# Seven block products for eight in the first two batches, behind the attention of all four

## The chip, the cores and the metric

The kernel runs on one core of one Trainium2 chip. The metric is the time of one execution on the device in microseconds (us), as the median of several runs. TensorE is called PE below, its weight loads PEld, VectorE DVE, ScalarE ACT, GpSimd POOL; SP (SyncE) issues the DMAs.

## What is computed

Three layers in a row, in float32: attention with a sigmoid in the softmax's place (4 batches, 12 heads, 448 positions, head width 64), a gated layer, and a layer with `h - tanh(h)`:

```python
scores = np.matmul(q, k.transpose(0, 1, 3, 2)) / 8 - np.log(448)
x = np.matmul(1 / (1 + np.exp(-scores)), v)        # as [1792 tokens, 768]
xn = x / np.sqrt(np.mean(x * x, -1) + 1e-6) * rms_g
g = xn @ w_gate                                    # 768 -> 1536
y = (g / (1 + np.exp(-g)) * (xn @ w_val)) @ w_out  # 1536 -> 768
h = y @ w_in2                                      # 768 -> 2048
out = (h - np.tanh(h)) @ w_out2                    # 2048 -> 768
```

The weights come as 64-bit floats.

## The kernel before, in words

Activations lie with features on the 128 partitions and the 448 tokens of a batch in the free dimension, one "unit" of 128 x 448 floats per chunk of features. Phase A is `w_gate` ("Ag") and `w_val` ("Av"), B is `w_out`, C is `w_in2`, D is `w_out2`. A float32 operand is split into a rounded part h (float32r) and the rest l, and a product is three matmuls hh + hl + lh of 128 x 128 weights and 448 columns. A **job** is one DMA of six 128 x 128 weight blocks (`jobs`, L285 to L339).

Batches 0 and 1 run all four phases first, then batches 2 and 3 (`BATCHES`). In the first half every job takes raw weights from memory (`load`, L349), rebuilds float32 out of the two halves of a 64-bit number (`fields`, `join`, L464 to L474), splits them (L479, L483) and stores them for the second half (`put`, L488). Phases A and C of the first half are plain block products for each batch (`job_units`, L925): 1440 matmuls. In the second half, A and C take two batches and two output chunks together in Strassen's manner with Winograd's sums (`seven_units`, L871): seven products of half the depth, each in a PSUM bank of its own, where the plain way has eight; DVE adds the banks into SBUF units (`plus`, L879; `done`, L884). That is 1260 matmuls. B and D are plain in both halves; their inner dimension is done in groups of four chunks (`GR`), and after each group DVE adds the bank to a sum that is held in SBUF (L829 to L835).

Attention: in batches 0 and 1 two heads go as a pair, values as plain float32 matmuls on the float32 sigmoids (`pair_av`, L616). In batches 2 and 3 each sigmoid is written to PSUM, split by ACT and DVE into h and l (`head_parts`, L652), and multiplied in seven float32r matmuls a head (`head_av`, L668). Batch 0's attention stands first; batch 1's runs beside the first jobs of batch 0, those of batches 2 and 3 beside the rest of the first half (`beside`, L1049).

The order on each engine is set by a planner (`Plan`, L61): work is listed with its reads, writes and a cost per engine, and is placed in time greedily, oldest first among what can start within `SOON` of the earliest. Buffers are slots of pools with a limit per kind (L240). Each engine runs its list in order, so a row that waits holds up the rows behind it. PSUM has 8 banks.

Of the kernel before, what the change touches and what calls it, by code (L numbers as in the profile page):

```python
# [8 lines left out]
F32 = mybir.dt.float32  # L9
# [12 lines left out]
P = 128  # L22
KM, KF1, KF2 = DM // P, FF1 // P, FF2 // P
EPS = 1e-6
NB = 6
ALONE = 3
GR = 4
# [4 lines left out]
N_WARM = 7  # L32
LOADS = [5, 6]
BEHIND = 2
MM = 190
SOON = 300
WINDOW = 500
N_UNIT, N_MOE, N_RAW, N_WT = 83, 44, 2, 7
N_AGAIN = 4
BACK = 3  # L40
BATCHES = ((0, 1), (2, 3))
# [3 lines left out]
ORDER_1_OUT = [(k, m) for g in range(KF1 // GR) for m in range(KM) for k in range(g * GR, (g + 1) * GR)]  # L45
ORDER_2 = [(k, m) for m in range(KF2) for k in range(KM)]
ORDER_2_OUT = [(k, m) for g in range(KF2 // GR) for m in range(KM) for k in range(g * GR, (g + 1) * GR)]
# [13 lines left out]
class Plan:  # L61
# [5 lines left out]
    WINDOW = WINDOW  # L67

    def __init__(self, room):
        self.room, self.work = room, []  # L70

    def add(self, engines, run, reads=(), writes=(), stream=None, after=0):

        n = len(self.work)
        self.work.append((engines, run, tuple(reads), tuple(writes), stream, after))
        for s, _ in (*reads, *writes):
            if not s.uses or s.uses[-1] != n:
                s.uses.append(n)

    def issue(self):  # L80
# [70 lines left out]
        while len(issued) < n_work:  # L151
# [3 lines left out]
            for n in waiting:  # L155
# [3 lines left out]
                if stream and streams[stream][stream_at[stream]] != n:  # L159
                    continue  # L160
                t_place = places(n)
# [15 lines left out]
            finish, start, n, e, ns, uses_port = min((c for c in cands if c[1] <= soonest), key=lambda c: c[2])  # L177
# [33 lines left out]
def tile_sigmoid_attention_moe_moe(  # L211
# [21 lines left out]
    cv_p = ctx.enter_context(tc.tile_pool(name="cv", bufs=2))  # L233
    v_p = ctx.enter_context(tc.tile_pool(name="v", bufs=2))
# [6 lines left out]
        "unit": (N_UNIT, {"moe": N_MOE, "kept": 24, "a": 40, "s": 14, "qk": 8, "qkr": 4, "acc": 12, "x": 12, "tmp_m": 8, "tmp_a": 4, "sq": 2, "rstd": 3,  # L241
                          "xs": 42, "tmp_s": 8, "tmp_x": 8}),
        "wt": (N_WT, {"raw": N_RAW, "whl": N_WT - N_RAW, "again": N_AGAIN, "op": 4}),
        "cv": (2, {"cv": 2}),
        "v": (2, {"v": 2}),
# [21 lines left out]
    def act(n, psum=False, ptr=False):  # L267
        return {"ACT": ((51 if psum else 93) + n / 1.2 + 93 * ptr, False)}

    def dve(n, two=True, psum=True, fast=False):  # L270
        return {"DVE": (66 + n / 0.96 / (2 if fast else 1), fast or (two and not psum))}

    def pool(n):
        return {"POOL": (110 + n * 2.16, True)}
# [4 lines left out]
    g_sb = const.tile([P, KM], F32, name="g_sb")  # L279
    id_sb = const.tile([TK, TK], F32, name="id_sb")  # L280
# [5 lines left out]

    def job(ph, bs, src, i, order):
        jobs.append((ph, bs, src, i, order[i * NB:(i + 1) * NB]))

    def group_a(bs, ms):  # L290
        for m in ms:
            job("Ag", bs, w_gate, m, ORDER_1)
            job("Av", bs, w_val, m, ORDER_1)

    def group_c(bs, ms):
        for m in ms:
            job("C", bs, w_in2, m, ORDER_2)

    PG = KM * GR // NB
    PAIRS = {"Ag": (w_gate, "A"), "Av": (w_val, "A"), "C": (w_in2, "C")}  # L300

    def second(ph, bs, g):
        for i in range(g * PG, (g + 1) * PG):
            job(ph, bs, *((w_out, i, ORDER_1_OUT) if ph == "B" else (w_out2, i, ORDER_2_OUT)))


    bs = BATCHES[0]
    for b in bs:
        group_a((b,), range(ALONE))
    group_a(bs, range(ALONE, GR))  # L310
    for g in range(KF1 // GR):
        ahead = range((g + 1) * GR, min((g + 2) * GR, KF1))
        group_a(bs, ahead[:1])
        second("B", bs, g)
        group_a(bs, ahead[1:])
    group_c(bs, range(GR))
    for g in range(KF2 // GR):
        ahead = range((g + 1) * GR, min((g + 2) * GR, KF2))
        group_c(bs, ahead[:1])
        second("D", bs, g)  # L320
        group_c(bs, ahead[1:])
# [810 lines left out]
```

## Time and profile before

| | us |
|---|---|
| median of 3 runs (1142.49 to 1144.13) | 1143.16 |
| the profiled execution | 1141.8 |
| its span, first to last instruction | 1140.0 |
| PE busy | 1123.2 |
| DVE busy | 759.7 |
| ACT busy | 407.0 |
| POOL busy | 173.0 |

A busy PE is one that has a matmul in flight. The stretches of the span: to 66 us batch 0's attention, to 126 us batch 1's with the first products, to 604 us the other two attentions among the first half's products, to 673 us the rest of phase D of batches 0 and 1, then the second half.

### The profile page before, as it was taken

Reading aid. Unit: us, or ns where it says so; the run is one execution under the profiler, and the core shown is the slowest. Engines: PE = TensorE matmul, PEld = TensorE weight load, DVE = VectorE, ACT = ScalarE, POOL = GpSimd, SP = SyncE. Lnnn points to the kernel's source line nnn. Section 1 sums busy time; section 2 is a strip of 40 time slices with the busy share of each in tenths; the row PEclk is TensorE's granted clock in tenths of the full one; section 3 lists DMA queues with packets and bytes.
Section 4 is the critical chain, followed back from the end, with each engine's and each line's share of the span. In section 5 each row is a group of like instructions: output and inputs, shape, how many; then the busy total and the mean of one; then the engine's idle time right before and its main releaser. Section 6 shows DMA issues by size and latency. Waiting matters only on the chain.

```text
span 1140.0 us, 15501 instructions
## 1 busy us (share of the span) xinstructions
PE 1123.2 (99%) x5706; PEld 986.9 (87%) x5706; DVE 759.7 (67%) x1303; ACT 406.9 (36%) x760; POOL 173.0 (15%) x136
## 2 busy tenths in 40 slices
PE   8999999999999999999999999999999999999998
PEld 5456788989889899898999899999999899999987
DVE  3576966675675987677575978738648897455542
ACT  4776534344443554444432422212202333212100
POOL 0001110121121221010121310111202302121200
PEclk9999999999999999999999999999999999999999
DMA  6778747666666575656549454424434434343322
GB/s 180 224 226 272 273 146 237 228 221 228 217 203 240 173 239 196 223 211 224 177 169 303 152 177 157 158 94 158 145 113 143 146 125 139 117 156 116 125 84 97
DMA packets 85245, 205.56 MB, mean 180 GB/s; under 512 B 11825, under 2 KB 49841, under 8 KB 85169
## 3 DMA queue, kind: packets, MB, share of 16 engines
q1 hardware_dynamic: 85168, 204.57, 53.8%
q8 instruction: 45, 0.74, 0.3%
q14 instruction: 32, 0.25, 0.1%
HBM read 134.93 MB, written 69.60 MB: 179 GB/s over the span
## 4 chain that ended last, share of the span: by engine, by line
PE 90%; DVE 3%; DMA 2%; SPq 2%; ACT 1%; issue 1%; POOL 0%; DVEq 0%; ACTq 0%; POOLq 0%
PE ps L953 60%; PE ps L909 21%; PE ps L587 4%; SPq L534 2%; DMA unit<-in_qkt 1%; PE ps L681 1%; PE ps L680 1%; PE ps L626 1%; DMA wt<-in_w_gate 1%; DVE unit L808 0%; PE ps L678 0%; DMA wt<-in_w_val 0%; DVE unit L755 0%; PE ps L630 0%; ACT unit L277 0%
## 5 line engine op out<-in xcount | busy, mean ns | idle before, releaser
L953 PE MATMUL ps<-unit,wt 128*128 128x448 f32 x3240 | 670.1, 366 | 2.5 <-DVE unit L277 1.5
L953 PEld LDWEIGHTS ps<-unit,wt 128*128 128x128 f32 x3240 | 605.5, 188 | 59.8 <-issue 5.9
L909 PE MATMUL ps<-unit,wt 128*128 128x448 f32 x1260 | 256.9, 365 | 0.0
L909 PEld LDWEIGHTS ps<-unit,wt 128*128 128x128 f32 x1260 | 236.4, 188 | 19.3
L277 ACT CAST wt<-cv 128x384 fp32r<-128x384 f32 (+1 forms) x81 | 50.3, 628 | 207.3 <-POOL cv L408 54.0
L835 DVE TENSOR_TENSOR unit<-ps,unit 128x448 f32<-128x448 f32 x120 | 69.4, 617 | 77.0 <-PE ps L953 76.6
L881 DVE TENSOR_TENSOR unit<-ps,unit 128x448 f32<-128x448 f32 x140 | 83.1, 619 | 38.1 <-PE ps L909 36.7
L277 ACT COPY unit<-ps 128x448 f32<-128x448 f32 (+1 forms) x78 | 41.1, 533 | 182.3 <-PE ps L909 61.9
L485 POOL TENSOR_TENSOR wt<-cv,wt 128x768 fp32r<-128x768 f32 x29 | 56.1, 1934 | 262.4 <-DVE wt L277 77.8
L277 ACT CAST unit<-unit 128x448 fp32r<-128x448 f32 (+1 forms) x125 | 66.8, 566 | 63.5 <-DVE unit L775 14.2
L808 DVE TENSOR_TENSOR unit<-unit 128x448 fp32r<-128x448 f32 x110 | 80.0, 739 | 8.8 <-ACT unit L277 6.1
L587 PE MATMUL ps<-unit 64*128 64x448 f32 (+1 forms) x576 | 74.2, 392 | 3.3 <-DVE unit L277 2.5
L472 DVE SCALAR_TENSOR_TENSOR cv<-wt,zero 128x768 uint32<-128x768 uint32 x68 | 67.7, 996 | 11.3 <-POOL wt L485 8.4
L666 DVE TENSOR_TENSOR unit<-ps,unit 128x448 fp32r<-128x448 f32 (+1 forms) x96 | 57.8, 619 | 23.5 <-ACT unit L277 18.1
L587 PEld LDWEIGHTS ps<-unit 64*128 64x128 f32 (+1 forms) x576 | 50.1, 179 | 25.5 <-issue 10.6
L277 DVE CAST wt<-cv 128x768 fp32r<-128x768 f32 (+1 forms) x61 | 29.2, 478 | 61.4 <-PE ps L953 51.7
L597 ACT ACTIVATE ps<-ps 128x448 f32<-128x448 f32 (+1 forms) x96 | 48.4, 527 | 46.8 <-PE ps L587 46.7
L277 ACT CAST zero<-wt 128x768 f16<-128x768 bf16 x41 | 44.2, 1077 | 43.1 <-DMA wt<-in_w_out 12.3
L953 PE MATMUL ps<-unit 128*128 128x448 f32 x216 | 50.1, 380 | 2.9 <-DVE unit L759 1.6
L277 DVE CAST unit<-unit 128x448 fp32r<-128x448 f32 (+1 forms) x90 | 35.1, 390 | 22.9 <-DMA unit<-in_qkt 14.3
L953 PEld LDWEIGHTS ps<-unit 128*128 128x128 f32 x216 | 39.5, 188 | 12.1 <-issue 5.0
L597 ACT ACTIVATE unit<-ps 128x448 f32<-128x448 f32 (+1 forms) x96 | 45.5, 540 | 4.5 <-PE ps L587 3.7
(80 smaller groups left out, 789.9 us busy)
## 6 DMA issues: line engine op xcount, KB each, us to landing
wt<-in_w_out SPq DMA_DIRECT2D x28, 768.0 KB, 5.4
wt<-in_w_in SPq DMA_DIRECT2D x16, 768.0 KB, 4.8
wD<-wt SPq DMA_DIRECT2D x32, 384.0 KB, 2.3
wt<-wD SPq DMA_DIRECT2D x16, 768.0 KB, 4.3
wt<-in_w_gate SPq DMA_DIRECT2D x12, 768.0 KB, 5.0
wt<-in_w_val SPq DMA_DIRECT2D x12, 768.0 KB, 6.2
wB<-wt SPq DMA_DIRECT2D x24, 384.0 KB, 2.4
wt<-wB SPq DMA_DIRECT2D x12, 768.0 KB, 4.3
```

Of the source, the lines that this page charges most:

```text
L277: add(engines, lambda e: (nc.scalar.copy if e == "ACT" else nc.vector.tensor_copy)(to(), of()), reads, writes)
L472: add(dve(NW, psum=False), lambda e: nc.vector.scalar_tensor_tensor(out=c.tile, in0=r.tile[:, :NW, 1], scalar=13, in1=z.tile, op0=ALU.logi ...
L485: add({**dve(wide, psum=False), **pool(wide)}, lambda e, q=q: ENG[e].tensor_sub(ap(q, "l"), f32(q), ap(q, "h").bitcast(F32)), [c["l"], c[" ...
L534: add({"SP": (1.4 * (hi - lo), False)}, lambda e, of=of, rows=rows, at=at: nc.sync.dma_start(out=t[w].tile[rows, lo:hi], in_=of[:, at:at + ...
L587: nc.tensor.matmul(ps[i, c].tile[:n, :S], lhsT=f[w].tile[rows, c * P:c * P + n], rhs=f[q].tile[rows, :], start=(w, q) == ("kh", "qh"), sto ...
L597: add(act(S, psum=True), lambda e: nc.scalar.activation(to.tile[at:at + n, :S], ps.tile[:n, :S], AF.Sigmoid, bias=-math.log(S), scale=1.0 ...
L666: add(dve(S), lambda e: nc.vector.tensor_sub(lo(), sv(), hi().bitcast(F32)), [ps["t"], kh], [kl])
L808: add({**pool(S), **dve(S, psum=False)}, lambda e: ENG[e].tensor_sub(c["l"].tile, t.tile, c["h"].tile.bitcast(F32)), [t["t"], kh], [kl])
L835: add(dve(S), lambda e: nc.vector.tensor_add(a.tile, psv(), a.tile), [ps["t"], a["t"]], [a["t"]])
L881: add(dve(S), lambda e: nc.vector.tensor_add(t.tile, banks[n].tile[:, :S], x.tile), [banks[n]["t"], x["t"]], [t["t"]])
L909: nc.tensor.matmul(ps.tile[:, :S], lhsT=part(a), rhs=x[b].tile, start=i == 0 and q == 0, stop=i == 2 and q == 2)
L953: nc.tensor.matmul(ps.tile[:, :S], lhsT=wt, rhs=a[p].tile, start=first and i == 0, stop=last and i == 2,)
```

## The change

A and C of batches 0 and 1 are done with seven products too. The attention of all four batches stands ahead of the products, all of it in pairs with float32 values (the h and l split of sigmoids is gone); the first products are mixed in with its last batch. The weights of the first half are stored as float32 together with the sums S1 to S4, and read back unsplit in the second half.

The seven products of a job share three banks, x, y and z (`CHAIN`). The first product is copied by ACT or DVE from bank x to bank y, and products 6, 7 and 4 are added on to bank x by TensorE itself, 2 on to y, 3 on to z. Between 1 and 6, 6 and 7, 7 and 4 the bank is copied out. Products 4 and 3 of a job are held back behind the first product of the next job (`held`). `Silu` takes the place of `Sigmoid` and a multiplication. B now has two groups of six chunks; the sum of a group goes by DMA to memory, comes back by DMA, and is copied into the PSUM bank on which the next group adds (`prologue`, `seed`, `epilogue`).

```diff
-GR = 4
+GR = {"B": 6, "D": 4}
-MM = 190
+MM = 203
-N_UNIT, N_MOE, N_RAW, N_WT = 83, 44, 2, 7
+N_UNIT, N_MOE, N_RAW, N_WT, N_CV = 74, 40, 3, 9, 3
...
+    def whole_bank(ps):
+
+        nc.tensor.matmul(ps[:, :S], lhsT=mark[:, :P], rhs=mark, start=True, stop=True)
...
+    def prologue(ph, bs, m, g):
+        for b in bs:
+            ps = ps_t[ph, b, m] = bank("m2")
+            if g:
+                d, a = sums_t.pop((ph, b, m)), unit("acc")
+                add({"SP": (650, False)}, lambda e, a=a, d=d: nc.sync.dma_start(out=a.tile, in_=d.tile), [d["t"]], [a["t"]], after=2000)
+                seed(ps, a, False)
+
+    def seed(to, of, psum):
+        copy({**act(S, psum=psum), **dve(S)}, lambda: to.tile[:, :S], lambda: of.tile[:, :S], [of["t"]], [to["t"]])
...
+            add(act(S, psum=psum), lambda e: nc.scalar.activation(sg.tile, of(), AF.Silu), [x["t"]], [sg["t"]])
...
+    CHAIN = {1: "x", 6: "x", 7: "x", 4: "x", 2: "y", 5: "z", 3: "z"}
...
         def done(n):
-            if n == 1:
-                u = f["p"] = unit("tmp_s")
-                copy(act(S, psum=True), lambda: u.tile, lambda: banks[1].tile[:, :S], [banks[1]["t"]], [u["t"]])
-            elif n == 6:
-                f["u"] = plus(6, f["p"])
+            if n == 1 and not opening:
+                seed(banks["y"], banks["x"], True)
+            elif n in (1, 6):
+                f[n] = copied()
             elif n == 7:
-                f["v"] = plus(7, f["u"])
-                c22 = plus(5, f["v"])
-                plus(5, f["u"], f["u"])
-                out(1, 1, c22)
+                out(1, 1, plus("z", copied()))
+            elif n == 2 and opening:
+                out(0, 0, plus("y", f[1]))
             elif n == 2:
-                out(0, 0, plus(2, f["p"], f["p"]))
+                out(0, 0, banks["y"], True)
             elif n == 4:
-                out(1, 0, plus(4, f["v"], f["v"]))
+                out(1, 0, banks["x"], True)
             elif n == 3:
-                out(0, 1, plus(3, f["u"], f["u"]))
+                out(0, 1, plus("z", f[6]))
...
+    mixed(attn_units(0))
+    mixed(attn_units(1), [lambda: norm(0), lambda: spread_norm(0)])
+    mixed(attn_units(2), [lambda: norm(1), lambda: spread_norm(1), *x_units(BATCHES[0], False)])
+    for j in range(AHEAD):
+        load(j)
+    mixed(attn_units(3), [lambda: norm(2)], [u for j in range(AHEAD) for u in (*conv(j), lambda j=j: load(j + AHEAD))])
+    norm(3)
```

Where the instructions stand. On PE, from the end of the first half's attention on; before (L953 is a plain product, L680, L681 and L678 the values of one head, L909 a seven-product matmul):

```order
L678 MATMUL ps<-unit,vs 128x448
L953 MATMUL ps<-unit,wt 128x448 x72
L723 MATMUL ps<-ones,unit 112x1 x4
L953 MATMUL ps<-unit,wt 128x448 x18
L733 MATMUL ps<-dg,ones 128x112 x4
L953 MATMUL ps<-unit,wt 128x448 x234
L909 MATMUL ps<-unit,wt 128x448 x315
L953 MATMUL ps<-unit,wt 128x448 x144
```

and now (L768 is a seven-product matmul, L803 a plain one, L555 the values of a pair):

```order
L555 MATMUL ps<-unit,vs 128x448
L768 MATMUL ps<-unit,wt 128x448 x12
L588 MATMUL ps<-ones,unit 112x1 x4
L768 MATMUL ps<-unit,wt 128x448 x3
L285 LDWEIGHTS mark
L285 MATMUL ps<-mark 128x448
L768 MATMUL ps<-unit,wt 128x448 x252
L803 MATMUL ps<-unit,wt 128x448 x6
L768 MATMUL ps<-unit,wt 128x448 x18
L803 MATMUL ps<-unit,wt 128x448 x210
```

The attention before ended close to the end of the first half's phase D; now it ends ahead of nearly all products, and all of A and C are in sevens: 2520 rows of L768 in place of 1260 of L909.

On ACT, in the attention of a batch of the second half; before (L597 is a sigmoid, L277 a copy or split, L817 the sigmoid of Ag):

```order
L597 ACTIVATE ps<-ps 128x448
L277 CAST unit<-ps 128x448
L597 ACTIVATE ps<-ps 128x448
L277 CAST unit<-ps 128x448
L597 ACTIVATE ps<-ps 128x448 x2
L277 CAST unit<-ps 128x448
L817 ACTIVATE unit<-ps 128x448 x2
```

and now, in batch 3 (L522 is a sigmoid, L712 the Silu of Ag, L569 a square):

```order
L712 ACT_TABLE_LOAD
L712 ACTIVATE unit<-unit 128x448
L278 CAST wt<-cv 128x384
L522 ACT_TABLE_LOAD
L522 ACTIVATE unit<-ps 128x448 x4
L278 CAST zero<-wt 128x768
L278 COPY unit<-ps 128x448
L569 ACTIVATE unit<-unit 128x448
L522 ACTIVATE unit<-ps 128x448 x2
L522 ACTIVATE unit<-ps 64x448 x2
L712 ACT_TABLE_LOAD
L712 ACTIVATE unit<-unit 128x448
```

The split of each sigmoid is gone from ACT, and function tables are loaded when it goes from Sigmoid to Silu and back, nine times in all; before, one load served the kernel.

On ACT, at the last C job and the first blocks of the last group of D of batches 0 and 1; before (L825 is Tanh):

```order
L825 ACTIVATE unit_4420<-ps_4329 128x448
L825 ACTIVATE unit_4424<-ps_4330 128x448
L277 CAST unit_4427<-unit_3526 128x448
L277 CAST zero0_85<-wt_4399 128x768
L277 CAST unit_4462<-unit_4424 128x448
```

and now (L719 is Tanh, `ps_6262` and `ps_6310` the banks x and y of the job, `zero_83<-wt` the first step on raw weights):

```order
L278 COPY ps_6310<-ps_6262 128x448
L278 COPY ps_6316<-unit_6248 128x448
L278 COPY ps_6322<-unit_6256 128x448
L278 COPY ps_6329<-unit_6283 128x448
L278 COPY ps_6333<-unit_6287 128x448
L278 COPY ps_6338<-unit_6291 128x448
L278 COPY unit_6352<-ps_6262 128x448
L719 ACTIVATE unit_6369<-ps_6310 128x448
L278 CAST unit_6390<-unit_6369 128x448
L278 COPY ps_6394<-unit_6294 128x448
L278 CAST zero_83<-wt_6350 128x768
```

ACT now also carries the copies within the chain of banks and the sums that come back for D, in one list with the steps that wait for raw weights.

## Rows read from the trace of the kernel before

**Rows 1.** The page: busy us of each engine, share of the span, instructions.

```profile
PE 1123.2 (99%) x5706; PEld 986.9 (87%) x5706; DVE 759.7 (67%) x1303; ACT 406.9 (36%) x760; POOL 173.0 (15%) x136
```

**Rows 2.** The page: share of the span on the chain that ended last, by engine.

```profile
PE 90%; DVE 3%; DMA 2%; SPq 2%; ACT 1%; issue 1%; POOL 0%; DVEq 0%; ACTq 0%; POOLq 0%
```

**Rows 3.** Waits of PE: for whom, us in total, times, longest us.

```profile
PE ps L587 <- DVE unit L277: 2.5, 2, 1.7
PE ps L626 <- ACT unit L597: 2.4, 1, 2.4
PE ps L1007 <- POOL ones L1003: 1.7, 1, 1.7
...
PE ps L587 <- ACT unit L597: 0.2, 1, 0.2
```

**Rows 4.** Chain of waits in order of time: start us, us, what.

```profile
604.60 14.53 PE ps L953 x72
...
673.24 63.80 PE ps L909 x315
```

**Rows 5.** Timeline of PE, batch 0's attention: start us, us, what, [idle before <-releaser].

```profile
20.09 2.72 PE L587 MATMUL ps<-unit 64*128 64x448 f32 x24
22.75 2.48 PE L626 MATMUL ps<-unit,vs 128*64 128x448 f32 x12
25.15 1.02 PE L630 MATMUL ps<-unit,vs 128*128 128x448 f32 x2
26.10 2.73 PE L587 MATMUL ps<-unit 64*128 64x448 f32 x24
31.26 4.08 PE L626 MATMUL ps<-unit,vs 128*64 128x448 f32 x12 [2.43 <-ACT unit L597]
```

**Rows 6.** Groups by line and shape: xcount | busy us, mean ns | idle us before, releasers.

```profile
L881 DVE TENSOR_TENSOR unit<-ps,unit 128x448 f32<-128x448 f32 x140 | 83.1, 619 | 38.1 <-PE ps L909 36.7
L808 DVE TENSOR_TENSOR unit<-unit 128x448 fp32r<-128x448 f32 x110 | 80.0, 739 | 8.8 <-ACT unit L277 6.1
L472 DVE SCALAR_TENSOR_TENSOR cv<-wt,zero 128x768 uint32<-128x768 uint32 x68 | 67.7, 996 | 11.3 <-POOL wt L485 8.4 <-ACT zero L277 1.7
...
L277 ACT COPY unit<-ps 128x448 f32<-128x448 f32 x59 | 31.0, 534 | 140.2 <-PE ps L909 61.9 <-PE ps L953 60.6 <-PE ps L630 12.6
...
L277 DVE COPY unit<-ps 128x448 f32<-128x448 f32 x21 | 13.1, 623 | 32.2 <-PE ps L953 31.1 <-PE ps L630 0.9
...
L860 DVE TENSOR_TENSOR unit<-unit 128x448 f32<-128x448 f32 x17 | 10.4, 621 | 5.6 <-ACT unit L859 5.5
...
L1008 ACT ACT_TABLE_LOAD x1 | 1.3, 1283 | 0.7 <-PEq L1117 0.7
```

**Rows 7.** Timeline of ACT, batch 0's attention: eight sigmoids of a pair.

```profile
21.25 3.81 ACT L597 ACTIVATE unit<-ps 128x448 f32<-128x448 f32 x8
```

**Rows 8.** Waits of ACT and DVE for raw weights: us in total, times, longest us.

```profile
ACT zero L277 <- DMA wt<-in_w_out: 12.3, 5, 5.8
...
ACT zero L277 <- DMA wt<-in_w_in: 7.0, 1, 7.0
```

**Rows 9.** Busy us (xinstructions) of each engine by stretch; then clock, DMA share, GB/s.

```profile
23.00:66.00 43.00, 39.53 (x244) 20.96 (x240) 26.30 (x54) 31.79 (x68) 2.17 (x2) 0.96 0.75 233
66.00:126.00 60.00, 58.02 (x307) 37.88 (x308) 42.98 (x77) 38.30 (x75) 8.15 (x6) 1.00 0.86 276
...
604.00:673.00 69.00, 67.99 (x343) 62.65 (x343) 54.99 (x91) 23.47 (x43) 18.33 (x13) 1.00 0.62 211
...
847.00:915.00 68.00, 67.50 (x332) 61.94 (x331) 54.67 (x98) 16.88 (x33) 15.32 (x13) 1.00 0.41 134
```

**Rows 10.** The page, DMA issues: xcount, KB each, median us from issue to landing.

```profile
wt<-in_w_in SPq DMA_DIRECT2D x16, 768.0 KB, 4.8
...
wC<-cv SPq DMA_DIRECT2D x16, 384.0 KB, 2.6
...
unit<-x SPq DMA_DIRECT2D x12, 224.0 KB, 5.0
```

More of the change, by code (lines that the diff above doesn't have):

```diff
@@ new lines, in tile_sigmoid_attention_moe_moe, with load @@
+    half = [j for j in range(len(jobs)) if jobs[j][1] == BATCHES[1]][0]
+    raws, whls, got, ops = {}, {}, {}, {}
+    stored = {}
+    NW, NH = NB * P, NB * P // 2
+    z = Slot(None, None)
+    z.tile = const.tile([P, NW], U32, name="zero")
+    nc.gpsimd.memset(z.tile, 0)
+    def load(j):
+        if j >= half:
+            return
+        ph, _, i, blocks = jobs[j]
+        flat = lambda t: t.bitcast(U16).rearrange("p n h -> p (n h)")
+        raws[j] = []
+        for src in ([SECOND[ph][0][i]] if blocks else [PAIRS[ph][0][2 * i + e] for e in range(2)]):
+            r = slot("raw", wt_p, [P, NW + 1, 2], U32, "wt")
+            raws[j].append(r)
+            add({"SP": (2200, False)}, lambda e, r=r, src=src: nc.sync.dma_start(
+                out=flat(r.tile)[:, 1:4 * NW + 1], in_=flat(src)), [], [r["t"]], after=2000)
@@ new lines, in fetch, with get @@
+    def fetch(j):
+        if not half <= j < len(jobs):
+            return
+        ph, _, i, blocks = jobs[j]
+        d = stored[ph, i]
+        def get(kind, pool, at, n, tag):
+            w = slot(kind, pool, [P, n * NW], F32, tag)
+            add({"SP": (1100 * n, False)}, lambda e: nc.sync.dma_start(
+                out=w.tile, in_=d.tile[:, at:at + n].rearrange("p n h -> p (n h)")),
+                [d[x] for x in range(at, at + n)], [w[x] for x in range(2 * n)], after=2000)
+            return w
+        got[j] = [get("cv", cv_p, 0, 1, "cv")] if blocks else [get("again", wt_p, at, 2, "wt") for at in (0, 2)]
@@ L871, in seven_units @@
     def seven_units(j):
-        ph, bs, _, p, _ = jobs[j]
-        banks = {n: bank("m2") for n in PRODUCTS}
+        ph, bs, p, _ = jobs[j]
+        opening = p == 0 and ph != "Av"
+        banks = {x: bank("m2") for x in "xyz"}
         fs = ops.pop(j)
         f = {}
-        out = lambda m, n, x: end(ph, bs[n], 2 * p + m, x)
-        def plus(n, x, to=None):
-            t = to or unit("tmp_s")
-            add(dve(S), lambda e: nc.vector.tensor_add(t.tile, banks[n].tile[:, :S], x.tile), [banks[n]["t"], x["t"]], [t["t"]])
+        out = lambda m, n, x, psum=False: end(ph, bs[n], 2 * p + m, x, psum)
```

702 lines of the change are left out of this document (268 added, 434 removed).

## The prediction

> **What bounds the kernel now.** I read the page's busy line first: PE has a matmul in flight for 1123.2 of 1140.0 us, the next engine, DVE, is busy for 759.7 [rows 1]. The chain that ended last says the same, 90% of it is PE [rows 2]. Then the waits of PE: ten groups, from 2.5 down to 0.2 us, 12.8 us in all [rows 3]; 4.8 of these are three groups before 14 us, for the first pair's operands and the warm-up's, and 0.5 lie in the second half. So nearly every matmul stands on the path, and the price of one is read from stretches of the chain that are nothing else: 72 plain products in 14.53 us (0.202 each), 315 seven-product matmuls in 63.80 (0.2025 each) [rows 4]. What takes matmuls away gains, as long as the other engines still deliver in time; the rest of the work is to see whether they do.
>
> **The sum, part by part,** against the profiled execution's own 1141.8 us; the median of the runs is 1.4 above it, and I add that at the end.
>
> Fewer products. A and C of batches 0 and 1 fall from 1440 matmuls to 1260: 180 x 0.2025 = 36.5 us less, all on the path.
>
> Values of batches 2 and 3. They leave 14 float32r matmuls a pair, 14 x 0.2025 = 2.84 us, for the paired float32 form: from 22.75 to 25.15 and on to 26.10, 3.35 us a pair [rows 5]. Twelve pairs: 6.2 us more. What goes from ACT and DVE with this (the split of every sigmoid) is off the path and gains nothing by itself.
>
> Waits that go. Of the 12.8 us of PE's waits, 7.5 lie between 14 and 673 us. The largest, 2.43 us at 31 us, is ACT behind q and k that compete with early raw weights, and the twelve matmuls behind it took 4.08 us where others took 2.48 (the mean clock of that stretch is 0.96, [rows 9]), 1.6 more. Those weights are now asked for behind the q and k of six pairs instead of four, and the hand-over from attention to the first products (the rest of the 7.5) is mixed in with attention. I take out 7.5 + 1.6 = 9.1 us, and price what comes in their place below.
>
> Small additions. Four matmuls over a whole bank after the norms: 0.8 us. The longer warm-up is covered by the first q and k, for which PE waits now; without that cover it is 16 x 0.2025 = 3.2 us, twice that at half the clock. Nothing for the last copies: a copy of 534 ns (ACT) or 623 (DVE) ends the kernel where an addition of 619 did [rows 6].
>
> So without new waits: 1141.8 - 36.5 + 6.2 - 9.1 + 0.8 = 1103.2 us.
>
> New waits, first: **function tables.** In batch 3's attention ACT goes nine times between Sigmoid and Silu; the planner's costs know nothing of it. The one load of before took 1283 ns [rows 6], so 11.5 us come on to ACT there. A pair costs PE 6.01 us (20.09 to 26.10, [rows 5]), and ACT 3.81 for eight sigmoids [rows 7] and some 1.1 for a copy and a square, 4.9. For the six pairs of batch 3 and 75 products mixed in, PE has 36 + 15 = 51 us, and ACT, by its list at these prices, about 41, with the loads 51. It is at its limit there, and the sigmoids free the banks of the scores. Bounds 0 (all in ACT's gaps) and 11.5 (all on the path); I take 4, since the shares are equal only at the end of the stretch and PE has products to do between. The Trainium skill speaks against this part: "ScalarE: Activation LUTs", What ACT_TABLE_LOAD costs, puts a switch at the load of 1283 ns and a drain of about 1380. The trace's load agrees with the first figure, and no row of before can show the second, since nothing was in flight at its only load; by the page ACT would carry 24 us instead of 11.5.
>
> Second: **the chain of banks.** Before, a bank of a seven-product job waited for its reader with seven other products still to go. Now product 6 must wait until product 1 has been copied out of bank x, 7 for the copy of 6, and 4 for that of 7, each with one other product of nine matmuls between: 9 x 0.2025 = 1.82 us, less the copy's 0.53, leaves 1.29 us. Queued ahead of these copies, on ACT and DVE, is the conversion of raw weights, which waits for its DMA. Before, the four largest groups of such waits made 37.3 us in 11 waits, 3.4 each [rows 8], and cost PE nothing. One of 3.4 us ahead of a copy now costs 3.4 - 1.29 = 2.1. Bounds: 0 if none falls so, 11 x 2.1 = 23 if all do. Three such copies, each with some 3 us of danger, in a job of 63 x 0.2025 = 12.8 us cover less than half of the time, and the third raw buffer makes waits rarer: I take a third, 7 us. The same copies in the second half have no raw weights ahead of them; its DVE has two thirds of the work of the first, and I price them at nothing.
>
> Sums of B and D through memory. Stored, loaded, copied into the bank: per pair of banks two copies more, and a pair of banks of D takes 24 matmuls, 4.9 us; the loads are listed several blocks ahead. On PE nothing; their load on ACT, DVE and DMA is in the rivals.
>
> 1103.2 + 4 + 7 = 1114.2, and with the median's 1.4: **1115 us**.
>
> **Rivals.** (a) Nothing new waits: 1103.2 + 1.4 = 1105. For it: the second half already ran seven products with 0.5 us of waits; against it, banks had more room there.
>
> (b) The tables lie on the path wholly: 1103.2 + 11.5 + 7 + 1.4 = 1123. With a drained ACT at each switch the same place costs more; eight sigmoids in 3.81 us are 0.48 each where a copy by itself takes 0.53 [rows 6, 7], so an emptied pipe shows as 0.06 us, not more, in these rows. The page's drain instead gives 1103.2 + 24 + 7 + 1.4 = 1136.
>
> (c) DVE becomes the bound in C and D of batches 0 and 1. By its list and the mean of each shape, DVE has 196 us of work there beside 219 us of PE (504 + 576 matmuls). Before, the fullest stretches had 54.99 of 69 and 54.67 of 68, 80%, at 1.0 and 0.5 us of PE's idle time [rows 9]; now it is 89%. The same addition in SBUF took 621 ns in one place and 739 in another where POOL ran beside it [rows 6]; with 85 of them at 739, 10 us come on top; and it waits 0.27 us for each bank it reads (38.1 us for 140), 14 us for 52 reads. 196 + 10 + 14 = 220: no gap is left, and every late DMA moves PE too. I price that at 12 us over the forecast, 1127.
>
> (d) Slower than before: DMA in the same stretch. Eight C jobs load two raw blocks of 0.786 MB and store four of 0.393 each, sixteen D jobs one and one, and 36 sums of 0.229 MB go out and come back: 25 + 19 + 16.5 = 60.6 MB [rows 10], in 219 us 277 GB/s. The trace has held 276 GB/s for 60 us at a DMA share of 0.86, but only 233 at 0.75 in another stretch [rows 9]. If 233 is all that this mixture gets, the stretch takes 260 us, 41 more: 1103.2 + 4 + 41 + 1.4 = 1150. It decides below 60.6 / (219 + 34.6) = 239 GB/s. Against it: 276 / 0.86 is 321 at full share.
>
> That the change does not do what it says is ruled out by the lists: 2520 rows of seven-product matmuls stand there.
>
> **How the numbers follow.** Forecast 0.54 (1106 to 1121); (a) 0.10; (b) 0.10, with the drain 0.04; (c) 0.15; (d) 0.07. From the low end, (a) less the warm-up's 3.2 us in case warm matmuls start sooner, 1101, to both bounds together, 1103.2 + 11.5 + 23 + 1.4 = 1139: 1101 to 1139 holds all but (d) and a little of (c). About 0.2% (2.3 us) is what a measurement of this kernel can tell from none. Faster by more than that has (a), (b), the drain, the forecast and nearly all of (c): 0.90; within it 0.03, at the far end of (c); slower 0.07, case (d).
>
> **What would show it.** In the trace after: batch 3's attention with nine loads, and gaps of PE behind sigmoids there of about 4 us in sum; a load's successor starting more than 0.1 us after it would speak for the drain. Waits of PE for ACT or DVE copies in A and C of the first half, some 7 us, behind conversions that waited for DMA; none in the second half. DVE busy for about 90% in C and D of the first half, DMA at about 280 GB/s. I am wrong if PE waits for more than 25 us there, if the seven-product matmuls run at another price than 0.2025, or if attention's 24 pairs take clearly more than 6 us each.

## The result, and the profile after

| | us |
|---|---|
| kernel before, median of 4 runs beside it | 1142.88 |
| changed kernel, median of 4 runs (1116.11 to 1117.91) | 1117.01 |
| ratio, 95% interval | 0.9772 (0.9755 to 0.9789) |
| profiled execution of the changed kernel | 1116.87 |
| its span | 1115.1 |

The change gains 26 us; the prediction was 1115 (1101 to 1139). The sum came out right, in part by luck: some 8 us that it did not price stand against some 5 that it had too high. Two of its terms were off, the cause given for a third was mostly another, and the experiments below show which.

The page's busy line, and the chain that ended last by engine, of the kernel after ([rows 1, 2] are those of before):

```profile
PE 1092.7 (98%) x5508; PEld 932.4 (84%) x5508; DVE 747.9 (67%) x1162; ACT 521.5 (47%) x917; POOL 153.4 (14%) x130
PE 92%; DVE 3%; ACT 2%; issue 1%; DMA 1%; SPq 1%; ACTq 0%; DVEq 0%
```

PE is still the bound, but with 22 us of its span idle for 17 before, on 198 matmuls less (5508 for 5706 on the two pages). PE's waits, the answer to [rows 3] (engine, line waited for: us in total, times, longest):

```profile
PE ps L768 <- DVE unit L742: 4.9, 4, 2.1
PE ps L512 <- DVE unit L278: 2.8, 1, 2.8
PE ps L285 <- POOL mark L834: 1.9, 1, 1.9
PE ps L512 <- ACT unit L278: 1.9, 2, 1.4
PE ps L768 <- ACT unit L278: 1.7, 3, 0.6
PE ps L768 <- DVE unit L278: 1.7, 3, 0.7
PE ps L551 <- ACT unit L522: 1.3, 1, 1.3
PE ps L803 <- ACT wt L278: 1.1, 1, 1.1
```

L768 are the seven-product matmuls, L803 those of B and D, L512 and L551 scores and values. L742 adds a bank (z, in a phase's first job also y) to a sum that is kept in SBUF, and so frees the bank; the kernel gives it to DVE alone. L278 is the common copy, L349 the split of weights. The largest group did not exist before. Where the waits lie (PE's timeline: start, us, line, count, and in brackets the idle time ahead and what ended it):

```profile
13.04 1.64 PE L512 MATMUL ps<-unit 64*128 64x448 f32 x12 [2.77 <-DVE unit L278]
115.84 0.47 PE L512 MATMUL ps<-unit 64*128 64x448 f32 x2 [1.35 <-ACT unit L278]
116.59 2.24 PE L512 MATMUL ps<-unit 64*128 64x448 f32 x10 [0.27 <-DVE unit L489]
158.40 2.48 PE L551 MATMUL ps<-unit,vs 128*64 128x448 f32 x12 [1.25 <-ACT unit L522]
430.86 3.71 PE L768 MATMUL ps<-unit,wt 128*128 128x448 f32 x10 [2.08 <-DVE unit L742]
446.76 9.39 PE L768 MATMUL ps<-unit,wt 128*128 128x448 f32 x45 [1.31 <-DVE unit L742]
802.11 40.50 PE L768 MATMUL ps<-unit,wt 128*128 128x448 f32 x198 [0.56 <-ACT unit L278]
```

Between 188 and 650 us PE waits 7.5 us in eight places: 4.9 us in four for L742, 0.9 in two for a copy out of bank x, 1.65 in two for splits of weights. In the second half it waits 2.5 us in four. Behind the waits at 115.8 and 430.9 matmuls run slowly for a while: the windows 115.80 to 122.20 and 430.80 to 434.60 have a granted clock of 0.73 and 0.57, means of its two levels (1.2 and 2.4 GHz). These windows and the stretches of the first half's products (columns: stretch and its us, then busy us with instructions of PE, weight loads, DVE, ACT, POOL, then PE clock, DMA share, GB/s):

```profile
115.80:122.20 6.40, 6.02 (x25) 2.50 (x25) 6.30 (x13) 4.37 (x9) 0.00 (x0) 0.73 0.28 78
430.80:434.60 3.80, 3.74 (x11) 3.35 (x12) 3.44 (x6) 2.81 (x6) 0.00 (x0) 0.57 0.84 271
188.00:440.00 252.00, 248.31 (x1204) 225.51 (x1204) 193.88 (x295) 111.36 (x177) 31.50 (x23) 0.99 0.64 222
440.00:650.00 210.00, 206.16 (x1005) 188.02 (x1004) 174.28 (x265) 106.61 (x178) 42.31 (x26) 1.00 0.80 282
```

In C and D (nearly all of the last row; C begins at 413.66) DVE is busy for 83%, where the prediction said about 90, and DMA moves 282 GB/s, where it said about 280. DVE's queue ahead of the wait at 430.86:

```profile
424.20 0.95 DVE L349 TENSOR_TENSOR wt<-cv,wt 128x768 fp32r<-128x768 f32 x1
425.07 2.21 DVE L384 TENSOR_TENSOR cv<-cv 128x384 f32<-128x384 f32 x4
427.19 0.95 DVE L349 TENSOR_TENSOR wt<-cv,wt 128x768 fp32r<-128x768 f32 x1
428.31 1.43 DVE L349 TENSOR_TENSOR wt<-cv,wt 128x768 fp32r<-128x768 f32 x2 [0.17 <-ACT wt L278]
429.66 1.15 DVE L742 TENSOR_TENSOR unit<-ps,unit 128x448 f32<-128x448 f32 x2
```

The additions that free bank z (L742) stand behind 5.5 us of splits (L349) and sums (L384) of weights, and none of these waits for a DMA: DVE works without a gap but 0.17 us. At 446.76 and 614.30 L742 stands behind splits and operands of activations, also without a DMA. That speaks against the cause that the prediction gave (copies behind conversions that wait for raw weights).

### The profile page after: what moved, and what is told of

It reads as the page before. It is cut to its first block, busy times and chain, and to the rows that moved or that the text cites. A ratio compares the mean times of both kernels' runs of the same rounds, so it can differ in the third digit from the quotient of the medians.

```text
span 1115.1 us, 15207 instructions
## 1 busy us (share of the span) xinstructions
PE 1092.7 (98%) x5508; PEld 932.4 (84%) x5508; DVE 747.9 (67%) x1162; ACT 521.5 (47%) x917; POOL 153.4 (14%) x130
## 4 chain that ended last, share of the span: by engine, by line
PE 92%; DVE 3%; ACT 2%; issue 1%; DMA 1%; SPq 1%; ACTq 0%; DVEq 0%
PE ps L768 43%; PE ps L803 37%; PE ps L512 5%; PE ps L551 5%; PE ps L555 2%; SPq L457 1%; DVE unit L278 1%; DVE wt L349 1%; ACT wt L278 1%; DVE unit L669 1%; DMA vs<-in_vt 1%; DVE unit L742 0%; PE ps L610 0%; DVE unit L715 0%; PE ps L588 0%
## 5 line engine op out<-in xcount | busy, mean ns | idle before, releaser
L768 PE MATMUL ps<-unit,wt 128*128 128x448 f32 x2520 | 526.9, 368 | 9.0 <-DVE unit L742 4.9
L768 PEld LDWEIGHTS ps<-unit,wt 128*128 128x128 f32 x2520 | 472.0, 188 | 58.5 <-DVE unit L742 6.4
L803 PE MATMUL ps<-unit,wt 128*128 128x448 f32 x2016 | 415.2, 366 | 1.1 <-ACT wt L278 1.1
L803 PEld LDWEIGHTS ps<-unit,wt 128*128 128x128 f32 x2016 | 378.2, 188 | 34.2 <-ACT wt L278 1.5
L278 ACT COPY unit<-ps 128x448 f32<-128x448 f32 x172 | 91.3, 534 | 320.9 <-PE ps L803 200.5
L278 DVE COPY unit<-ps 128x448 f32<-128x448 f32 x80 | 49.9, 624 | 124.8 <-PE ps L803 118.6
L349 DVE TENSOR_TENSOR wt<-cv,wt 128x768 fp32r<-128x768 f32 (+1 forms) x108 | 100.0, 932 | 16.8 <-ACT wt L278 15.2
L522 ACT ACTIVATE unit<-ps 128x448 f32<-128x448 f32 x192 | 91.0, 541 | 6.1 <-PE ps L512 5.1
L278 ACT CAST wt<-cv 128x768 fp32r<-128x768 f32 (+1 forms) x91 | 70.5, 781 | 40.9 <-DVE cv L338 17.1
L349 POOL TENSOR_TENSOR wt<-cv,wt 128x768 fp32r<-128x768 f32 (+1 forms) x28 | 52.5, 1875 | 194.0 <-ACT wt L278 102.0
L278 ACT CAST unit<-unit 128x448 fp32r<-128x448 f32 (+1 forms) x112 | 62.4, 566 | 30.7 <-DVE unit L715 8.9
L278 DVE CAST unit<-unit 128x448 fp32r<-128x448 f32 (+1 forms) x133 | 59.2, 445 | 25.2 <-DMA unit<-in_qkt 19.9
L512 PE MATMUL ps<-unit 64*128 64x448 f32 (+1 forms) x576 | 70.2, 379 | 5.1 <-DVE unit L278 2.8
L349 POOL TENSOR_TENSOR wt<-wt 128x768 fp32r<-128x768 f32 (+1 forms) x21 | 36.6, 1745 | 269.9 <-ACT wt L278 189.2
L742 DVE TENSOR_TENSOR unit<-ps,unit 128x448 f32<-128x448 f32 x84 | 52.0, 620 | 32.3 <-PE ps L768 22.6
L512 PEld LDWEIGHTS ps<-unit 64*128 64x128 f32 (+1 forms) x576 | 49.1, 172 | 28.8 <-issue 15.7
L278 ACT CAST wt<-wt 128x768 fp32r<-128x768 f32 (+1 forms) x60 | 44.8, 754 | 53.9 <-PE ps L768 38.1
L551 PE MATMUL ps<-unit,vs 128*64 128x448 f32 x288 | 60.4, 555 | 1.3 <-ACT unit L522 1.3
L278 ACT CAST zero<-wt 128x768 f16<-128x768 bf16 x46 | 49.7, 1081 | 21.4 <-DVE cv L338 14.9
L349 DVE TENSOR_TENSOR wt<-wt 128x768 fp32r<-128x768 f32 (+1 forms) x59 | 51.4, 880 | 6.3 <-ACT wt L278 5.4
```

The lines of the kernel that those rows point to most:

```text
L278: add(engines, lambda e: (nc.scalar.copy if e == "ACT" else nc.vector.tensor_copy)(to(), of()), reads, writes)
L349: add({**dve(n, psum=False), **pool(n)}, lambda e: ENG[e].tensor_sub(lo(), of(), hi().bitcast(F32)), [*reads, *kh], [*kl])
L512: nc.tensor.matmul(ps[i, c].tile[:n, :S], lhsT=f[w].tile[rows, c * P:c * P + n], rhs=f[q].tile[rows, :], start=(w, q) == ("kh", "qh"), sto ...
L522: add(act(S, psum=True), lambda e: nc.scalar.activation(to.tile[at:at + n, :S], ps.tile[:n, :S], AF.Sigmoid, bias=-math.log(S), scale=1.0 ...
L551: nc.tensor.matmul(ps.tile[i * D:(i + 1) * D, :S], lhsT=v.tile[:, c, i, :], rhs=a.tile, start=(c == 0), stop=False)
L742: add(dve(S), lambda e: nc.vector.tensor_add(t.tile, ps.tile[:, :S], t.tile), [ps["t"], t["t"]], [t["t"]])
```

## Experiments

All beside runs of the kernel before; "against the changed kernel" is the difference of the two ratios times 1143, uncertain by some 2.5 us (3.5 to 4 for the stores doubled and the copies to ACT), so that the smaller ones are read at their place in the trace.

| run | median us | ratio (95%) | against the changed kernel |
|---|---|---|---|
| eight products | 1142.44 | 0.9994 (0.9982 to 1.0005) | +25.4 |
| own banks | 1128.88 | 0.9874 (0.9856 to 0.9893) | +11.7 |
| no weight sums | 1107.93 | 0.9688 (0.9672 to 0.9704) | -9.6 |
| stores doubled | 1147.18 | 1.0037 (1.0010 to 1.0063) | +30.3 |
| one table | 1114.92 | 0.9757 (0.9744 to 0.9770) | -1.7 |
| seven warm-ups | 1117.58 | 0.9782 (0.9768 to 0.9795) | +1.1 |
| priority | 1118.53 | 0.9786 (0.9773 to 0.9799) | +1.6 |
| early q, k; four value buffers | 1112.21 | 0.9739 (0.9726 to 0.9752) | -3.8 |
| the same, copies to ACT, 400 ns | 1105.79 | 0.9666 (0.9637 to 0.9695) | -12.1 |
| the same, copies to ACT, 800 ns | 1109.97 | 0.9692 (0.9668 to 0.9717) | -9.1 |
| kernel before, late weights | 1143.53 | 0.9998 (0.9981 to 1.0014) | (0 against before) |

### What the products are worth

```diff
-                2: ("A12", "B21"), 4: ("A22", "T4"), 3: ("S4", "B22")}
+                2: ("A12", "B21"), 4: ("A22", "T4"), 3: ("S4", "B22"), 8: ("S1", "T1")}
...
+        if bs == BATCHES[0]:
+            at = order.index((7, 0))
+            order[at:at] = [(8, i) for i in range(3)]
```

> The changed kernel with one product of nine matmuls (S1 by T1, on to bank z) added to each of the 20 seven-product jobs of batches 0 and 1, so that these jobs have eight again: 180 matmuls more, and an output that is not the reference's. Theory of the prediction (every matmul is on the path): 180 x 0.2025 = +36.5 us, about 1153.5. Rival (in the first half something other than TensorE sets the pace): the added time would only fill waits that are there, 7.5 us and 2.4 us of slow clock behind them, so +27 us or less.

25.4 us, by the rival. With the eighth product PE's waits after 14 us are 6.3 us for the changed kernel's 12.9; between 188 and 650 us three are left, of 2.2 for 7.5, and L742 is down to one:

```profile
PE ps L768 <- ACT unit L278: 3.3, 5, 1.2
PE ps L768 <- DVE unit L278: 0.7, 1, 0.7
PE ps L768 <- DVE unit L742: 0.6, 1, 0.6
```

So of 36.5 us that go with the products 6.6 come back as waits and 1.8 as slow clock behind the longest of them; the other 2.7, about the comparison's uncertainty, are not accounted for. The term -36.5 and a price for new waits belong together: the waits are there because the products are gone.

### The chain of banks itself

```diff
-    CHAIN = {1: "x", 6: "x", 7: "x", 4: "x", 2: "y", 5: "z", 3: "z"}
+    CHAIN = {n: n for n in PRODUCTS}
...
+            elif n == 6:
+                f["u"] = plus(6, f["p"])
+            elif n == 7:
+                f["v"] = plus(7, f["u"])
+                c22 = plus(5, f["v"])
+                plus(5, f["u"], f["u"])
+                out(1, 1, c22)
```

(In the opening job of a phase one sum is overwritten ahead of its second use; the work is the same.)

> The changed kernel with its chain of banks undone: each of the seven products has a bank of its own, and DVE adds them in SBUF, as the second half of the kernel before did. Theory of the prediction (products wait because a bank must be copied out before the next product is added on to it): 7 us less, about 1110. Rival from the trace after (DVE has too much queued in the first half): six additions a job for two, some 50 us more on DVE in the first half where it has 368 of 462 us, so the waits grow and the time goes up by 5 to 20 us.

11.7 us more: the prediction's sign was wrong, undoing the chain costs. C and D hold 943 matmul records for 1005 in the same 210 us, and PE waits there for split weights:

```profile
PE ps L799 <- ACT wt L278: 8.0, 2, 4.3
PE ps L799 <- DVE wt L278: 3.2, 2, 1.6
```

```profile
440.00:650.00 210.00, 198.17 (x943) 178.72 (x942) 169.52 (x271) 101.10 (x168) 45.83 (x33) 0.98 0.76 270
```

Ahead of the longest of these waits (4.27 us, to 460.78) ACT's split stands behind a tanh that waits for an addition on DVE (L737):

```profile
458.98 0.58 ACT L719 ACTIVATE unit<-unit 128x448 f32<-128x448 f32 x1 [3.21 <-DVE unit L737]
459.90 0.83 ACT L278 CAST wt<-cv 128x768 fp32r<-128x768 f32 x1 [0.34 <-DVE cv L338]
```

So additions on DVE put off the splits of weights, and with these the matmuls that read them. Letting PE add in the bank keeps nearly half of the change's gain.

### DVE's amount, its order, or the raw weights

Less work on DVE, with every DMA left in place:

```diff
-            t = slot("cv", cv_p, [P, NW], F32, "cv")
-            a11, a12, a21, a22 = ((x, n) for x in c for n in range(2))
-            total(t, 0, a21, a22, sub=False)
-            total(t, 1, (t, 0), a11)
-            total(c[0], 0, a11, a21)
-            total(c[0], 1, a12, (t, 1))
-            c.append(t)
+            c.append(c[1])
```

> The changed kernel without the four sums of weights of each job of batches 0 and 1: S1 and S2 are taken from the second raw block, S3 and S4 from the first, so the output is not the reference's. DMAs, splits and products stay. 20 x 4 operations of 128 x 384 go from DVE and GpSimd, about 0.63 us each, 50 us in all. Rival from the trace after (DVE's backlog makes TensorE wait in the first half, 7.5 us of waits and 2.4 us of slow clock behind them): 5 to 10 us less. Theory of the prediction (the copies stand behind conversions that wait for raw weights from memory): within 2 us of the changed kernel, waits of 6 us or more stay between 188 and 650 us.

9.6 us less. L742 is gone from the list of waits; two are left between 188 and 650 us:

```profile
420.44 13.87 PE L762 MATMUL ps<-unit,wt 128*128 128x448 f32 x67 [0.62 <-ACT unit L278]
620.85 14.94 PE L797 MATMUL ps<-unit,wt 128*128 128x448 f32 x72 [1.15 <-ACT wt L278]
```

DVE is busy for 341 us between 188 and 650, for 368 in the changed kernel. The raw weights still come by the same DMAs, and ACT and DVE even wait longer for them there (20.4 us for 7.4), so they are not the cause. (The sums also held one of the three `cv` buffers, which is free here; the copies moved to ACT in the last experiments leave these buffers alone.) Is it the order of DVE's queue, then?

```diff
             if i == 2:
+                was, plan.later = plan.later, -100
                 done(n)
+                plan.later = was
```

> The changed kernel with the work behind a finished product (copies of bank x, additions on banks y and z, what follows them) put 100 places ahead in the planner's rank, so that DVE and ACT take it before conversions and splits of weights; nothing else is changed. If TensorE's waits of the first half come of the order in DVE's queue, 7.5 us of waits and 2.4 of slow clock shrink to a third: 4 to 8 us less. If they come of the amount of work on DVE, or conversions become late for their job in turn, within 2 us or more time, with waits that move to the lines that read weights (L803, or L768 behind wt).

No gain (+1.6, not to be told from none), and the waits moved: L742 has left the list, and two waits as long as all of the first half's are in its place.

```profile
429.75 4.43 PE L768 MATMUL ps<-unit,wt 128*128 128x448 f32 x13 [3.81 <-DVE wt L349]
612.66 3.73 PE L768 MATMUL ps<-unit,wt 128*128 128x448 f32 x9 [4.28 <-DVE unit L278]
```

The first is as the second theory has it: what is put ahead of the splits makes the splits late. The second is for a copy out of a bank, at 611.98 on DVE, and DVE had stood idle shortly before it, for raw weights:

```profile
605.30 0.62 DVE L278 CAST zero<-wt 128x768 f16<-128x768 bf16 x1 [5.07 <-DMA wt<-in_w_out]
```

So the mechanism of the prediction exists: in this order it costs PE 4.28 us, and in the changed kernel no wait of the first half comes of it. This run shows that the order alone gains nothing; that the amount counts is shown by the run before it and by the last experiments.

### Function tables

```diff
-            add(act(S, psum=psum), lambda e: nc.scalar.activation(sg.tile, of(), AF.Silu), [x["t"]], [sg["t"]])
+            add(act(S, psum=psum), lambda e: nc.scalar.activation(sg.tile, of(), AF.Sigmoid), [x["t"]], [sg["t"]])
```

> The changed kernel with Sigmoid in the place of Silu: ACT keeps one table for the whole of attention and the first products, and the nine loads in batch 3's attention go. It leaves out the multiplication by the gate's value, so the output is not the reference's. Theory of the prediction (4 us of the loads on the path): 4 us less, about 1113; bounds 0 and 11.5 less. Reading of the trace after (one wait of 1.25 us behind a load): 1 to 2 us less. By a drain of 1.4 us at each switch on the path: 24 us less. In the trace the wait of 1.25 us at 158 us is gone.

1.7 us less in the comparison, and the wait of 1.25 us at 158 us is gone from the trace (the twelve matmuls of L551 follow without idle time); no other wait of attention was behind a load. In the changed kernel eight of the nine loads stand in batch 3's attention and one at 203.84 us. Between 137.6 and 188 us ACT is busy for 40.94 of 50.40 us with the eight in it, so it had room for them. Its timeline around the first:

```profile
143.39 1.95 ACT L522 ACTIVATE unit<-ps 128x448 f32<-128x448 f32 x4
145.36 1.28 ACT L712 ACT_TABLE_LOAD   x1
146.66 0.58 ACT L712 ACTIVATE unit<-unit 128x448 f32<-128x448 f32 x1
```

The load starts 0.02 us after the last sigmoid and the next operation 0.02 us after the load. The rule of the Trainium skill that the prediction weighed ("ScalarE: Activation LUTs", What ACT_TABLE_LOAD costs) is borne out in the load, 1.28 us, and not in the drain of 1.38: no such gap stands on either side of any of the nine.

### The start, and the early weights

```diff
-N_WARM = 16
+N_WARM = 7
```

> The changed kernel with seven warm-up matmuls for sixteen, as before the change. Theory of the prediction (the longer warm-up is covered, worth nothing): within 1 us. Reading of the trace after (scores find the clock up, 18 matmuls in 2.43 us where 3.88 were needed, and the third half pair starts at 17.97 for 20.09): 1.5 to 2.5 us more, all of it before 20 us.

The prediction's nought holds (+1.1, not to be told from none). In the profile before the fourth half pair of batch 0 (twelve matmuls of scores; the expectation calls it the third) starts at 20.09 us, in the changed kernel's at 17.97, and with seven warm-ups at 17.88. What stands ahead of it, with seven warm-ups (PE's timeline):

```profile
12.95 1.64 PE L512 MATMUL ps<-unit 64*128 64x448 f32 x12 [1.50 <-DVE unit L278]
14.53 2.48 PE L551 MATMUL ps<-unit,vs 128*64 128x448 f32 x12
```

So the 2.1 us are not the longer warm-up's. The same places of the kernel before, which the rows ahead of the prediction do not hold:

```profile
13.52 2.61 PE L587 MATMUL ps<-unit 64*128 64x448 f32 x12 [1.73 <-DVE unit L277]
16.06 3.15 PE L626 MATMUL ps<-unit,vs 128*64 128x448 f32 x12
```

Operands 0.6 us later, and 24 matmuls 1.6 us slower, in this one execution: the next run keeps the old warm-up and takes 1.66 and 2.48 us for them. Four other runs with sixteen warm-ups and the same work up to here (eight products, own banks, no weight sums, priority) take 2.43 to 2.61 us for the twelve matmuls of scores, in windows with a granted clock of 0.50 to 0.55, so nearly all at the lower level; the changed kernel takes 1.64 at 1.00. So the clock at this place differs between executions of the same work.

```diff
-LOADS = [5, 6]
+LOADS = [9, 10]
```

> The kernel before with its first two raw-weight loads issued four half pairs later (behind the q and k of six pairs, as the change has them), nothing else changed. Theory of the prediction (the wait of 2.43 us at 31 us and the slow clock behind it, 1.6 us, come of q and k that compete with the early weights): 4.0 us less than the kernel before, a ratio of 0.9965. Rival: the wait has another cause, or comes back when the first products find their weights late: within 1 us.

No difference: the rival. The wait at 31 us and the slow matmuls behind it are gone, the fourth half pair starts at 17.68, and PE was 6.5 us ahead by 42 us (35.72 for 42.23). Then it stood where the profile before had no idle time, for batch 0's norm and for the first products:

```profile
51.48 0.92 PE L723 MATMUL ps<-ones,unit 128*112 128x1 f32 x8 [2.26 <-DVE unit L708]
59.96 1.12 PE L733 MATMUL ps<-dg,ones 112*128 112x112 f32 x8 [2.19 <-DVE dg L728]
65.99 2.70 PE L953 MATMUL ps<-unit 128*128 128x448 f32 x12 [1.48 <-ACT unit L597]
```

The first products start at 65.99 here and at 66.03 in the profile before. On DVE, the norm's work (L737) stands behind a conversion that waits for raw weights; here, and the same conversion in the profile before:

```profile
56.66 0.61 DVE L277 CAST zero<-wt 128x768 f16<-128x768 bf16 x1 [5.32 <-DMA wt<-in_w_val]
58.17 0.15 DVE L737 TENSOR_SCALAR ms<-ps 112x4 f32<-112x4 f32 x1
```

```profile
57.13 0.61 DVE L277 CAST zero<-wt 128x768 f16<-128x768 bf16 x1 [2.21 <-DMA wt<-in_w_val]
```

These weights land only half a microsecond earlier, so PE's lead ahead of that place is worth nothing.

### How near DMA is

```diff
+        d2 = Slot(None, lambda: dram_p.tile([P, NW], F32, name=d.tile.name + f"_{at}b"))
+        add({"SP": (1100, False)}, lambda e: nc.sync.dma_start(out=d2.tile, in_=c.tile), [c[0], c[1]], [d2["t"]], after=2000)
```

> The changed kernel with every store of converted weights doubled (the second copy goes to memory that nobody reads): 48 x 0.393 = 18.9 MB more in C and D of batches 0 and 1, 59 MB to 78 in 210 us, and 23.6 MB more in A and B. It asks for rival (d), how near DMA is to being the bound. If 282 GB/s at a share of 0.80 can go to 352 at full share: 78 MB take 222 us, +12 us, and A and B stay. If the mixture has no more than about 282: +67 us. If DMA has room beyond that: 0 to +3 us.

30.3 us more, between the first two cases. A wait in PE's timeline; from the chain, the transfer that an earlier wait of this kind (to 546.3) ended with; and the windows of that stretch:

```profile
557.30 0.74 PE L805 MATMUL ps<-unit,wt 128*128 128x448 f32 x1 [4.55 <-ACT ps L278]
```

```profile
539.95 5.78 DMA unit<-sumD
```

```profile
490.00:540.00 50.00, 46.73 (x221) 42.42 (x220) 41.12 (x62) 21.08 (x35) 5.74 (x3) 0.97 0.95 343
540.00:590.00 50.00, 40.20 (x180) 35.84 (x179) 30.31 (x47) 18.92 (x32) 4.13 (x3) 0.90 0.95 340
```

At a share of 0.95 this mixture moves 340 GB/s, and the sums of D that come back from memory are then late for their bank (17.6 us of waits of L805 for the copy into the bank). So rival (d) was a real limit at the wrong figure: 233 GB/s at a share of 0.75 left room, the limit lies near 340 for this mixture, and the changed kernel's 282 are below it. (The Trainium skill, "DMA: Bandwidth & Descriptors", Specifications, gives one core some 358 GB/s of HBM; these windows are 4 to 5% under it, and the one from 350 to 400 us of this run, with 369 GB/s at 0.98, is 3% over.) The sums through memory, which the prediction put at nothing, are what pays first. How much of that is the transfers and how much their place in SP's list, which the doubled stores lengthen, the run does not tell: a load of such a sum takes 5.3 us from issue to landing, for 4.8 in the changed kernel (medians).

### A kernel that beats both

```diff
-                add({"SP": (1.4 * (hi - lo), False)}, lambda e, of=of, rows=rows, at=at: nc.sync.dma_start(
+                add({"ACT" if (b, p) == (0, 1) else "SP": (600, False)}, lambda e, of=of, rows=rows, at=at: (nc.scalar if e == "ACT" else nc.sync).dma_start(
...
-    vs_p = ctx.enter_context(tc.tile_pool(name="vs", bufs=3))
+    vs_p = ctx.enter_context(tc.tile_pool(name="vs", bufs=4))
```

> The changed kernel with two edits meant to beat it: the six q and k transfers of the second pair are issued by ACT, which is idle from 2.3 to 7.3 us, for SP, which issues them from 6.45 to 10.1; and the value tiles have four buffers for three, so that SP does not stand before a value transfer with the next pair's q and k behind it at 107 to 115 us. By the trace after, the wait of 2.77 us at 10.3 us goes or shrinks to under 1, and the waits of 1.35 and 0.27 us at 115.8 with 2 us of slow clock behind them go: 3 to 6 us less. Rival: ACT's issues delay the first pair's own operands, or the next wait takes the place (the score banks behind sigmoids): within 1.5 us.

3.8 us less, within the first theory's 3 to 6, but in one of its two places: the wait of 2.77 us at the start is gone (the fourth half pair starts at 15.99), while the one in batch 2 stayed, at 114.20 us with 2.18 for 1.35 + 0.27. SP no longer stands there for a value buffer; the chain ahead of it is ACT, with sigmoids and copies back to back, so the buffer was not its only cause. The slow matmuls behind it are gone in this execution: the granted clock is 1.00 from 114 to 121.

```diff
-                cands.append(min(ways, key=lambda w: (w[1], w[0])))
+                extra = 400 if self.spare is not None and n >= self.spare and "ACT" in engines else 0
+                cands.append(min(ways, key=lambda w: (w[1] + extra * (w[3] == "DVE"), w[0])))
```

> The kernel with early q and k and four value buffers (about 4.8 us faster than the changed one), and behind attention a copy or cast that DVE or ACT could do goes to DVE only if ACT would start it over 400 ns later: by the lists 133 of 335 such operations move from DVE to ACT. DVE has 368 of 462 us in the first half and ACT 218; at 0.55 us each some 60 us of DVE's load go there. If the amount of DVE's work sets the waits of the first half (7.5 us and 2.4 of slow clock): 4 to 9 us less than that kernel, about 1105. If the order or the DMAs set them: within 2 us of it, about 1112.

0.9666 for 0.9739: 8.3 us less than without it, as the amount of DVE's work asks, and 12.1 us (0.9666 / 0.9772, 1.1%) less than the changed kernel. The same windows as above, now with DVE at 336 us for 368 and ACT at 265 for 218, and 32 matmul records more in them:

```profile
188.00:440.00 252.00, 250.31 (x1224) 228.87 (x1224) 183.15 (x266) 141.40 (x225) 31.07 (x23) 1.00 0.65 226
440.00:650.00 210.00, 208.24 (x1017) 190.30 (x1016) 152.59 (x230) 123.45 (x213) 27.94 (x19) 1.00 0.83 288
```

DMA moves no less than before, 288 GB/s, and the waits of that half are 3.4 us with the one at 643.7.

> As the kernel with 400 ns, with 800 ns: 221 of 335 operations move from DVE to ACT, which then has about 340 of 462 us in the first half and DVE 270. If DVE's amount sets the waits and ACT has room: 5 to 9 us less than with neither, about 1105. If ACT's queue is late in its turn: slower than the kernel with 400 ns by 2 us or more, with waits of TensorE for ACT L278.

Twice the penalty gives 1109.97; its interval overlaps with that of 400 ns, so the two are not told apart. Behind attention its waits point to the second theory: 5.8 us in six waits for ACT's copies (L279 in these two kernels) where 400 ns has 2.4 in three. But its profiled execution is the slowest of five, and 5.7 us of its delay stand ahead of 154 us, where the two kernels have the same operations in the same order: at 81.31 PE waits 2.91 us for DVE, which stood 5.39 us for a store to land, for 2.36 with 400 ns.

## Why the prediction was right, and where it was not

- **The sum.** The profiled execution took 1116.87 us where the sum, without the median's 1.4, had 1114.2. Over it: 3.8 us in batch 2, 1.8 of slow clock in the first half, 2.0 in waits of before that were misread and waits of the second half, 0.5 in the chain. Under it: 2.75 of the tables, and 2.1 because the one profile of before had a slow start. That these nearly cancel is luck; 0.6 us stay open.
- **Fewer products, -36.5.** 180 matmuls at the price of [rows 4] hold within 1%: the longest rows after are 0.2045 (198 in 40.50). The eighth product put back is worth 25.4, because waits go with it.
- **Values, +6.2.** The pairs of batches 0 and 1 take 6.01 us as in [rows 5], and those of batch 2 have the same matmuls (L551, L555), 2.48 and 1.02 us where nothing waits. No run takes this part alone.
- **Waits that go, -9.1.** The term is 1.0 too large: 1.5 us of the waits of before lie in the second half (0.50 at 888.04 and 1.00 at 1108.77), not 0.5, so that 6.5 + 1.6 could go. They went, but the reason for the largest piece fell: later weights alone gain nothing in the kernel before, since the norm's work on DVE stands behind the conversion of weights that land no sooner. In the changed kernel batch 0's norm stands inside batch 1's attention and the first products in batch 3's; that this is what keeps the lead there is a reading that no run tests.
- **Tables, +4.** Mis-sized: one wait of 1.25 us, 1.7 us in the comparison (not to be told from none). The step that failed is that ACT would be at its limit, with 51 us of work beside PE's 51: it is busy for 40.94 of 50.40 us.
- **Chain of banks, +7.** 7.5 us of waits came, in the stretch named, and the mechanism was mostly another. Not bank x behind conversions that wait for DMA (0.9 us are for a copy out of bank x, at 366.95 and 421.90, and not behind such a conversion), but above all banks behind work that DVE is busy with (4.9 us for L742), the mechanism of rival (c) at the forecast's size. The waits for raw weights on which the price rested had shrunk, from 37.3 us in the four groups of before to 7.4 on ACT and DVE in the first half's products. Undoing the chain costs 11.7.
- **Slow clock behind new waits.** Not in the sum: 1.8 us behind the longest of the first half (63 matmuls from 430.86 in 14.59 us) and some 2 in batch 2. The expectations count 2.4 in the first half, with 72 matmuls from 631.00 in 15.18 us; these are 0.6 over the price at a granted clock of 1.00, and why is open.
- **Batch 2.** Not priced: 1.6 us of waits and those 2 of slow clock at 115.8, where batch 0's operands are made beside attention.
- **Second half, 0.** 2.5 us in four waits of 0.5 to 0.7, each of product 7 for the copy of product 6 out of bank x: the mechanism of the forecast, where it was priced at nothing. In two of the four (at 680.92 and 802.11) the copy stands on ACT behind a cast of weights that had waited for DVE's split:

```profile
679.61 0.83 ACT L278 CAST wt<-wt 128x768 fp32r<-128x768 f32 x1 [3.81 <-DVE wt L349]
680.35 0.53 ACT L278 COPY unit<-ps 128x448 f32<-128x448 f32 x1
```

- **Warm-up, 0.** Right; what looked like a gain of 2.1 us at the start was in the one profile of before.
- **Rivals.** (b) and its drain are refuted by ACT's rows; (c) is the mechanism that is there, though DVE is not full (193 us busy from 413.66 to 646.2, its list had 196, but in 232 us for 219), and it costs at most 7.5 + 1.8 us where 12 were to come on top of the forecast's 7; (d) has its figure wrong and its limit 20% further on; (a) needs a DVE with less to do, and the kernel with the copies on ACT and the two edits ahead of it comes to its time.

## What to carry to other kernels

Matmuls taken away are worth their price less the waits that they had covered; read the busiest second engine of that very stretch, and take work off it (copies to an idle engine, sums left to TensorE in the bank) along with the matmuls. Here, with DVE busy for 368 of 462 us, a new order of its queue only moved the waits; some 30 us less of work on it removed more than half of them. A wait in a single profile is a gain only if the next producer is early too: look at what the engine would wait for once it is ahead.

## What was not expected of the hardware

A DMA share of 0.95 with 340 GB/s is reached by this mixture of 0.2 to 0.8 MB transfers, while the 233 GB/s at 0.75 of [rows 9] were no limit. A table load follows an operation of ACT and is followed by one within 0.02 us. A wait of PE of 2.08 us was followed by matmuls at a granted clock of 0.57 for 3.8 us, so that a wait can cost nearly twice its length; but the same wait (2.08 us with one table, 2.13 with early q and k) was followed by a clock of 1.00 in the profiles of those two runs. What decides between the two is not shown.
